# Dividing block 0's first part among three engines, with its attention in the later units' form

## The chip, the cores and the metric

The kernel runs on one core of a Trainium2 chip. TensorE (PE) multiplies matrices, and its weight loads (PEld) run beside its matmuls; VectorE (DVE), ScalarE (ACT) and GpSimd (POOL) work element by element, and SyncE (SP) issues the DMAs. Each engine works through its own instructions in the order in which they stand, and waits on semaphores for the others. The metric is the device time of one execution in microseconds; lower is better.

## The reference

```python
scores = scale * q @ k.T            # 4 batches, 8 heads, 576 tokens, head size 64
scores = where((rel >= 0) & (rel < 64), scores, -1e9)
x = softmax(scores) @ v             # -> [2304 tokens, 512]
h = x @ w_in                        # 512 -> 2048
P = a[0] + a[1]*h + a[2]*h**2 + a[3]*h**3
Q = 1 + abs(b[0])*abs(h) + abs(b[1])*h**2
x = (P / (Q + 1e-6)) @ w_out        # 2048 -> 512
out = (sigmoid(x @ w_gate) * (x @ w_val)) @ w_out2   # 512 -> 1536 -> 512
```

## The kernel before

**Tiles and phases.** The 2304 tokens are five blocks of 512, 256, 512, 512 and 512. Attention is done in 18 units of 128 tokens, four for each full block; a unit makes two score tiles (`scores`), their row maxima (`peak`), exponentials (`exps`), sums' reciprocals (`inverse`) and products (`norm`), transposes them (`turn`, `turned`), multiplies by the values (`values`) and writes x in two parts (`x_hi`, `x_lo`). "Part 1" of a block is the rational layer (`step1`, 16 values of f of 128 hidden columns each), "part 2" the gated layer (`step2`, 12 values of f). The phases run in the order part 1 and part 2 of block 0, part 1 of blocks 1 and 2, part 2 of blocks 1 and 2, and the same for blocks 3 and 4.

**Two-part numbers.** Each fp32 operand is held as a rounded part `hi` and a remainder `lo`, and each product is three matmuls (`mm3`). So a weight chunk of 128 x 512 is loaded raw (`load`, into one of three buffers of pool s) and converted once by six operations (`rescale`, `sign`, `shift`, `low_bits`, `hi`, `lo`), through a temporary `wt` in SBUF (pool t). Chunks that are needed again are stored to DRAM (`store`) and later reloaded. There are 32 chunks for part 1 (kinds i and o) and 36 for part 2 (g, v, p); pool w holds 28 at a time.

**Part 1, one f.** Twelve matmuls make `h` in one of two PSUM banks of pool h. Then come `size` and `cubic` (ACT), `slope`, `quad` (q is multiplied up), `horner` twice (DVE), `log` and `seed` (ACT), `check` (DVE), the Newton step (`newton` on DVE, or `rest` and `correct`), `ratio` (DVE), and `hi` and `lo` of the result `gs`; twelve matmuls (`product`) add it into four y banks.

**Order.** Nothing is placed by hand. Every step is given to a planner (`op`) with a priority, the engines that may do it with a cost for each (`ways`), and what it waits for; `order()` plays the program through with these costs and emits the instructions in the order that results. A cost marked `PORT` is one that the planner doesn't let overlap with another such cost on DVE or POOL. In the kernel before, most steps have two or three ways:

```python
Q = op(t0 + 1.97, [pool(n), dve(n)], quad, [Q], uses=[q_s, a_s])
X = op(t0 + 4.16, [act(n), dve2(n), pool1(n)], hi, [G], [gs_s], [g_s])
X = op(t0 + 3.61, [pool(n), dve(n)], lo, [X], uses=[gs_s, g_s])
```

**Block 0's attention.** Its four units keep q in a spare x tile and make scores from 64-row halves; later units keep q in a tile with zeros off the diagonal (`q_diag`), so that one matmul of 128 rows does for two halves. At the start the loads of q and k, of the first raw weights and, later, of v share SP's queue, in the order of the priorities.

Of the kernel before, what the change touches and what calls it, by code (L numbers as in the profile page):

```python
# [251 lines left out]
def tile_window_attention__rational_ffn__glu(  # L252
# [143 lines left out]
    def weights(c, prio, keys, again):  # L396
# [92 lines left out]
    def unit(u, t0, prio_load, prio_v):  # L489
# [37 lines left out]

        def mask_of(m):  # L530
            if first_block:
                assert (2 * u + 1) % (S // 64)
                name = "a" if 2 * u % (S // 64) == 0 else "n"
            else:
                name = "n" if (2 * u + m) % (S // 64) else "f"
            return masks[name][:, None, :].to_broadcast([P, HP, P])

        def scores(m):
            def go(e):
# [7 lines left out]
                r = slice(64 * m, 64 * m + 64)  # L547
                for i in range(HP):
                    if first_block:
                        parts = [  # L550
                            (t, z["q"][r, i, t], z["k"][r, i, t.start:t.start + P])
                            for t in (slice(0, 64), slice(64, P))
                        ]
                    else:
                        parts = [(slice(0, P), z["q"][:, 2 * i + m], z["k"][:, i, 64 * m:64 * m + P])]
                    for rows, lhs, rhs in parts:
                        nc.tensor.matmul(  # L557
                            p[rows, i * P:(i + 1) * P], lhs, rhs, start=not on_pe, stop=not on_pe or i == HP - 1
                        )
# [64 lines left out]
        def values(e):  # L624
            p = z["p"] = bank(v_s)
            for i in range(HP):
                for c in range(2):
# [86 lines left out]
    def step1(p, b, fs, f, t0):  # L714
# [366 lines left out]
```

## Time and profile before

| | |
|---|---|
| Time, three runs | 1024.28, 1024.69, 1024.74 us (median 1024.69) |
| The profiled execution: its time, its span | 1018.68 us, 1016.9 us |
| Busy in the span: PE, DVE, ACT, POOL | 960.3, 725.7, 484.8, 200.7 us |
| Moved by DMA | 170.92 MB, mean 168 GB/s |

The span is from the first to the last instruction of one profiled execution. Busy times are sums over stages that differ: the first 40 us are block 0's attention, from 40.5 us on part 1 of block 0 runs, the first matmuls of part 2 come at 204 us, and from about 400 us on PE is hardly ever idle.

### The profile page before, as it was taken

What the parts mean: (1) busy time and instruction counts of PE and PEld (TensorE: products, weight loads), DVE (VectorE), ACT (ScalarE), POOL (GpSimd) and SP (SyncE); (2) the same over time, 40 slices, a digit from 0 to 9 for tenths busy, and PEclk for the clock granted to TensorE, in tenths of its full rate; (3) what the DMA queues carried; (4) which work ended last, traced back from release to release, by engine and by line L of the source; (5) the groups of instructions that cost most, each with busy time, mean ns of one, the idle gap of its engine ahead of it and who ended that gap; (6) DMA issues with size and microseconds to landing.
All of it is one profiled execution on the core that took longest, in us unless ns stands there. A gap on an engine that the chain in (4) does not pass through costs nothing.

```text
span 1016.9 us, 14241 instructions
## 1 busy us (share of the span) xinstructions
PE 960.3 (94%) x5120; PEld 798.7 (79%) x5120; DVE 725.7 (71%) x1272; ACT 484.8 (48%) x974; POOL 200.7 (20%) x215
## 2 busy tenths in 40 slices
PE   8977777689999998999999999999999999999998
PEld 6855555468888996888998888888888888888886
DVE  5999899988888899886887765688998932222222
ACT  3775667445567874655443432565666610001001
POOL 3331232121313452231000110223232200000000
PEclk7998978699999998999999999999999999999999
DMA  9645655979999523556526675410155541005001
GB/s 291 233 145 210 245 206 197 336 257 313 318 313 345 184 68 107 197 193 223 161 63 218 211 221 179 145 63 1 47 181 188 193 158 63 1 21 186 1 1 41
DMA packets 72677, 170.92 MB, mean 168 GB/s; under 512 B 20704, under 2 KB 29920, under 8 KB 72608
## 3 DMA queue, kind: packets, MB, share of 16 engines
q1 hardware_dynamic: 72608, 170.03, 50.0%
q8 instruction: 40, 0.66, 0.3%
q14 instruction: 29, 0.24, 0.1%
HBM read 129.63 MB, written 40.37 MB: 167 GB/s over the span
## 4 chain that ended last, share of the span: by engine, by line
PE 78%; DVE 11%; DMA 6%; ACT 3%; issue 2%; POOL 0%; SPq 0%; DVEq 0%; ACTq 0%; POOLq 0%
PE h L705 29%; PE y L705 28%; PE a L705 14%; DMA wraw<-in_moe_w_out_dram 2%; DMA wraw<-in_moe_w_in_dram 2%; PE a L557 2%; DVE tg L751 2%; DVE wt L435 2%; PE a L630 1%; DVE tq L763 1%; DVE wt L430 1%; PE y L557 1%; DVE w L323 1%; PE a L380 1%; DMA qk<-in_k_dram 1%
## 5 line engine op out<-in xcount | busy, mean ns | idle before, releaser
L705 PE MATMUL h<-x,w 128*128 128x512 f32 (+1 forms) x1680 | 380.1, 376 | 15.0 <-ACT w L316 9.1
L705 PEld LDWEIGHTS h<-x,w 128*128 128x128 f32 x1680 | 299.9, 193 | 75.4 <-ACT w L316 11.7
L705 PE MATMUL y<-g,w 128*128 128x512 f32 (+1 forms) x960 | 225.9, 386 | 19.8 <-DVE g L323 11.8
L705 PEld LDWEIGHTS y<-g,w 128*128 128x128 f32 x960 | 176.0, 198 | 58.2 <-DVE g L323 14.6
L705 PE MATMUL a<-x,w 128*128 128x512 f32 (+1 forms) x720 | 160.2, 372 | 4.7 <-ACT sm L579 3.5
L705 PE MATMUL y<-w,g 128*128 128x512 f32 x648 | 158.6, 392 | 0.3 <-DVE w L323 0.3
L882 ACT ACTIVATE sg<-h 128x512 f32<-128x512 f32 (+1 forms) x60 | 33.3, 555 | 246.1 <-PE h L705 246.0
L705 PEld LDWEIGHTS a<-x,w 128*128 128x128 f32 x720 | 127.1, 190 | 28.8 <-ACT sm L579 3.9
L705 PEld LDWEIGHTS y<-w,g 128*128 128x128 f32 x648 | 120.0, 188 | 24.8 <-DVE w L323 0.6
L751 DVE SCALAR_TENSOR_TENSOR tg<-tg,ca_sb,h 128x512 f32<-128x512 f32 (+1 forms) x160 | 108.1, 688 | 24.4 <-ACT ta L730 16.6
L885 DVE TENSOR_TENSOR sg<-sg,a 128x512 f32<-128x512 f32 (+1 forms) x60 | 37.8, 633 | 121.7 <-PE a L705 118.8
L748 POOL TENSOR_TENSOR tq<-tq,ta 128x512 f32<-128x512 f32 (+1 forms) x62 | 80.4, 1299 | 123.0 <-ACT tq L739 121.5
L757 ACT ACTIVATE tr<-tq,biases 128x512 f32<-128x512 f32 (+1 forms) x80 | 54.3, 678 | 56.7 <-POOL tq L748 53.8
L734 ACT ACTIVATE tg<-h,ca_sb 128x512 f32<-128x512 f32 (+1 forms) x80 | 51.6, 645 | 52.9 <-PE h L705 52.6
L763 DVE SCALAR_TENSOR_TENSOR tq<-tq,tr 128x512 f32<-128x512 f32 (+1 forms) x80 | 54.2, 679 | 17.3 <-ACT tr L760 16.5
L427 POOL TENSOR_SCALAR wraw<-wraw 128x512 f32<-128x512 f32 x38 | 32.3, 849 | 163.4 <-ACT wt L414 151.5
L414 ACT ACTIVATE wt<-wraw 128x512 f32<-128x512 f32 x59 | 39.8, 674 | 49.0 <-DMA wraw<-in_moe_w_out_dram 24.5
L782 DVE SCALAR_TENSOR_TENSOR tg<-tg,ca_sb,tr 128x512 f32<-128x512 f32 (+1 forms) x80 | 61.9, 774 | 0.6
L768 DVE SCALAR_TENSOR_TENSOR tr<-tq,tr 128x512 f32<-128x512 f32 (+1 forms) x76 | 57.5, 760 | 0.2
L621 DVE STREAM_TRANSPOSE et<-sm 32x256 f32<-32x256 f32 x128 | 55.8, 436 | 2.3
L318 DVE CAST g<-sg 128x512 fp32r<-128x512 f32 (+1 forms) x42 | 17.1, 408 | 56.0 <-PE y L705 55.5
L760 ACT ACTIVATE tr<-tr,biases 128x512 f32<-128x512 f32 (+1 forms) x80 | 54.4, 680 | 1.8
(94 smaller groups left out, 957.0 us busy)
## 6 DMA issues: line engine op xcount, KB each, us to landing
w<-wo SPq DMA_DIRECT2D x32, 512.0 KB, 3.3
w<-wp SPq DMA_DIRECT2D x32, 512.0 KB, 3.3
wraw<-in_moe_w_out_dram SPq DMA_DIRECT2D x28, 512.0 KB, 4.7
w<-wg SPq DMA_DIRECT2D x28, 512.0 KB, 3.3
w<-wv SPq DMA_DIRECT2D x28, 512.0 KB, 3.3
w<-wi SPq DMA_DIRECT2D x20, 512.0 KB, 3.3
vv<-in_v_dram SPq DMA_DIRECT2D x35, 256.0 KB, 3.9
wraw<-in_moe_w_in_dram SPq DMA_DIRECT2D x16, 512.0 KB, 4.4
```

What stands on the lines that cost most here:

```text
L414: nc.scalar.activation(out=t.bitcast(F32), in_=x, func=AF.Copy, scale=REBIAS * REBIAS)
L621: nc.vector.transpose(out=to[cols, :, rows], in_=at[rows, :, cols])
L705: nc.tensor.matmul(p, lhs(a), rhs(b), start=first and n == 0, stop=last and n == 2)
L734: nc.scalar.activation(out=z["g"], in_=z["h"], func=AF.Copy, scale=ca_sb[:, 3:4])
L748: ENGINES[e].tensor_tensor(out=z["q"], in0=z["q"], in1=z["a"], op=ALU.mult)
L751: return lambda e: nc.vector.scalar_tensor_tensor(out=z["g"], in0=z["g"], scalar=ca_sb[:, m:m + 1], in1=z["h"], op0=ALU.add, op1=ALU.mult)
L757: nc.scalar.activation(out=z["r"], in_=z["q"], func=AF.Ln, scale=LN_SCALE, bias=lnb)
L760: nc.scalar.activation(out=z["r"], in_=z["r"], func=AF.Exp, scale=-1.0, bias=exb)
L763: nc.vector.scalar_tensor_tensor(out=z["q"], in0=z["q"], scalar=1.0 + 1e-6, in1=z["r"], op0=ALU.add, op1=ALU.mult)
L768: nc.vector.scalar_tensor_tensor(out=z["r"], in0=z["q"], scalar=2.0, in1=z["r"], op0=ALU.subtract, op1=ALU.mult, reverse0=True)
L782: nc.vector.scalar_tensor_tensor(out=z["g"], in0=z["g"], scalar=ca_sb[:, 0:1], in1=z["r"], op0=ALU.add, op1=ALU.mult)
L885: nc.vector.tensor_tensor(out=z["t"], in0=z["t"], in1=z["v"], op=ALU.mult)
```

## The change

Block 0's part 1 gets one engine for each step: `slope`, `rest` and `hi` on ACT, `quad`, `correct` and `lo` on POOL, and the Newton step is always `rest` and `correct`. The conversion of 24 of the 32 part-1 chunks (`banked`: kinds i and o from the ninth chunk on) uses a PSUM bank of pool a (two banks) as its temporary `wb` in place of `wt`, with `rescale` and `hi` on ACT, `sign` on POOL and the other three on DVE. Block 0's units take the form of the later ones, each with a tile `qd` of its own out of pool w that is cleared first; their q and k are loaded ahead of all weights, and their values go to y banks. A mask is dropped, the planner's cost of a wide matmul is raised, units of later blocks may not start before a given matmul of the phase before (`gates`), and the `hi` steps are kept in the order of f.

```diff
 def pe(n, count=1):
-    return ("PE", count * (n / 2400 + 0.0025))
+    return ("PE", count * (n / 2400 + (0.0135 if n > 256 else 0.0025)))
...
-        raw_s, t_s, w_s = Slot("s"), Slot("t"), Slot("w")
+        n = before.get("n", 0)
+        before["n"] = n + 1
+        banked = c[0] in "io" and n >= 8
+        raw_s, t_s, w_s = Slot("s"), Slot("a" if banked else "t"), Slot("w")
...
+        one, two = (dvep(512), [act(512, True)]) if banked else (dve(512), [act(512), dve2(512), pool1(512)])
         o = before["size"] = before["take"] = op(
-            prio, [act(512), dve2(512), pool1(512)], rescale, [o, before.get("size")], [t_s, w_s], [raw_s],
+            prio, two, rescale, [o, before.get("size")], [t_s, w_s], [raw_s],
...
-        o = op(prio, [pool1(512), dve2(512)], sign, [o], uses=[raw_s])
-        o = op(prio, [dve(512)], shift, [o], uses=[t_s, raw_s])
-        o = op(prio, [dve(512)], low_bits, [o], uses=[t_s, raw_s])
-        o = op(prio, [act(512), dve2(512), pool1(512)], hi, [o], uses=[t_s, w_s])
-        o = op(prio, [pool(512), dve(512)], lo, [o], uses=[t_s, w_s])
+        o = op(prio, [pool1(512)] if banked else [pool1(512), dve2(512)], sign, [o], uses=[raw_s])
+        o = op(prio, [one], shift, [o], uses=[t_s, raw_s])
+        o = op(prio, [one], low_bits, [o], uses=[t_s, raw_s])
+        o = op(prio, two, hi, [o], uses=[t_s, w_s])
+        o = op(prio, [one] if banked else [pool(512), dve(512)], lo, [o], uses=[t_s, w_s])
...
-        banks = ("y", "y", "h", "h", "a") if first_block else ("a",) * 5
+        banks = ("y", "y", "h", "h", "y") if first_block else ("a",) * 5
...
+        if first_block:
+            ready = op(-360 + u, [("NONE", 0.0)], take_q, [taken], [q_s])
+            zeros = op(-350 + u, [("DVE", 0.6, *PORT), ("POOL", 1.1, *PORT)], clear, [ready], uses=[q_s])
...
-        Q = op(t0 + 2.74, [dve2(n, 2), act(n, False, 2), pool1(n, 2)], slope, [A, coef], [q_s], [a_s])
-        Q = op(t0 + 1.97, [pool(n), dve(n)], quad, [Q], uses=[q_s, a_s])
+        Q = op(t0 + 2.74, [dve2(n, 2), act(n, False, 2), pool1(n, 2)] if b else [act(n, False, 2)], slope, [A, coef], [q_s], [a_s])
+        Q = op(t0 + 1.97, [pool(n), dve(n)] if b else [pool(n)], quad, [Q], uses=[q_s, a_s])
...
-        if b == 0 and f % 4 < 1:
-            Q = op(t0 + 0.6, [act(n, False, 1), dve2(n), pool1(n)], rest, [Q], uses=[q_s])
-            L = op(t0 + 2.52, [pool(n), dve(n)], correct, [Q], uses=[r_s, q_s])
+        if b == 0:
+            Q = op(t0 + 0.6, [act(n, False, 1)], rest, [Q], uses=[q_s])
+            L = op(t0 + 2.52, [pool(n)], correct, [Q], uses=[r_s, q_s])
...
-        X = op(t0 + 4.16, [act(n), dve2(n), pool1(n)], hi, [G], [gs_s], [g_s])
-        X = op(t0 + 3.61, [pool(n), dve(n)], lo, [X], uses=[gs_s, g_s])
+        X = prev_h["g"] = op(t0 + 4.16, [act(n), dve2(n), pool1(n)] if b else [act(n)], hi, [G], [gs_s], [g_s], prev_h.get("g"))
+        X = op(t0 + 3.61, [pool(n), dve(n)] if b else [pool(n)], lo, [X], uses=[gs_s, g_s])
...
-        unit(u, -40 + 3.48 * u, -200 + u, -200 + u + 8.94)
+        unit(u, -40 + 3.48 * u, -300 + u, -200 + u + 8.94)
```

What the planner makes of it shows in the order of the instructions. First DVE, in the middle of part 1 of block 0, before: `wt` and `w` are chunks being converted, `tg`, `tq` and `tr` the tiles of one f.

```order
163 L430 SCALAR_TENSOR_TENSOR wt<-wt,wraw 128x512
164 L748 TENSOR_TENSOR tq<-tq,ta 128x512
165 L435 SCALAR_TENSOR_TENSOR wt<-wraw,wt 128x512
166 L422 TENSOR_SCALAR wraw<-wraw 128x512
167 L318 CAST w<-wt 128x512
168 L430 SCALAR_TENSOR_TENSOR wt<-wt,wraw 128x512
169 L323 TENSOR_TENSOR w<-wt,w 128x512
170 L763 SCALAR_TENSOR_TENSOR tq<-tq,tr 128x512
171 L435 SCALAR_TENSOR_TENSOR wt<-wraw,wt 128x512
172 L782 SCALAR_TENSOR_TENSOR tg<-tg,ca_sb,tr 128x512
173 L768 SCALAR_TENSOR_TENSOR tr<-tq,tr 128x512
174 L323 TENSOR_TENSOR w<-wt,w 128x512
```

The same place on DVE after the change (lines are two lower):

```order
150 L749 SCALAR_TENSOR_TENSOR tg<-tg,ca_sb,h 128x512
151 L436 SCALAR_TENSOR_TENSOR wb<-wb,wraw 128x512
152 L749 SCALAR_TENSOR_TENSOR tg<-tg,ca_sb,h 128x512
153 L323 TENSOR_TENSOR w<-wb,w 128x512
154 L441 SCALAR_TENSOR_TENSOR wb<-wraw,wb 128x512
155 L780 SCALAR_TENSOR_TENSOR tg<-tg,ca_sb,tr 128x512
156 L323 TENSOR_TENSOR w<-wb,w 128x512
157 L436 SCALAR_TENSOR_TENSOR wb<-wb,wraw 128x512
158 L441 SCALAR_TENSOR_TENSOR wb<-wraw,wb 128x512
159 L761 SCALAR_TENSOR_TENSOR tq<-tq,tr 128x512
```

The Newton step, the remainder of `gs`, `quad` and the signs have left DVE, and the conversions read and write a PSUM bank (`wb`); ten rows make one f. Counted over the rows before part 1's result is split for part 2, DVE has 309 instructions before and 260 after, and 38 chunks are converted in both.

Next POOL, in the same part of the program, before:

```order
38 L427 TENSOR_SCALAR wraw<-wraw 128x512 x3
39 L748 TENSOR_TENSOR tq<-tq,ta 128x512
40 L427 TENSOR_SCALAR wraw<-wraw 128x512 x3
41 L748 TENSOR_TENSOR tq<-tq,ta 128x512
42 L427 TENSOR_SCALAR wraw<-wraw 128x512 x3
```

And after:

```order
73 L746 TENSOR_TENSOR tq<-tq,ta 128x512
74 L433 TENSOR_SCALAR wraw<-wraw 128x512
75 L323 TENSOR_TENSOR g<-tg,g 128x512
76 L433 TENSOR_SCALAR wraw<-wraw 128x512
77 L746 TENSOR_TENSOR tq<-tq,ta 128x512
78 L777 TENSOR_TENSOR tr<-tq,tr 128x512
79 L433 TENSOR_SCALAR wraw<-wraw 128x512 x2
80 L777 TENSOR_TENSOR tr<-tq,tr 128x512
81 L323 TENSOR_TENSOR g<-tg,g 128x512
```

POOL's share of two values of f was one `quad` and three signs; it is now two each of `quad`, `correct` and `lo`, and four signs.

Last SP, at the program's start, before:

```order
1 L405 DMA wraw<-in_moe_w_in_dram 128x1024
2 L510 DMA q_144<-in_q_dram 128x512
3 L511 DMA qk<-in_k_dram 128x4x128
4 L405 DMA wraw<-in_moe_w_in_dram 128x1024
5 L510 DMA qk<-in_q_dram 128x512
6 L511 DMA qk<-in_k_dram 128x4x128
```

And after:

```order
1 L515 DMA qd<-in_q_dram 64x8x64 x2
2 L517 DMA qk<-in_k_dram 128x4x128
3 L515 DMA qd<-in_q_dram 64x8x64 x2
4 L517 DMA qk<-in_k_dram 128x4x128
5 L515 DMA qd<-in_q_dram 64x8x64 x2
6 L517 DMA qk<-in_k_dram 128x4x128
7 L515 DMA qd<-in_q_dram 64x8x64 x2
8 L517 DMA qk<-in_k_dram 128x4x128
9 L411 DMA wraw<-in_moe_w_in_dram 128x1024 x3
```

Each q is now two DMAs of 64 rows, and the first three weight chunks stand behind all twelve loads of q and k.

## Rows read from the trace of the kernel before

**Rows 1.** Stretches: us; busy PE, PEld, DVE, ACT, POOL; granted clock, DMA share, GB/s.

```profile
0.00:40.40 40.40, 37.08 (x385) 30.83 (x386) 28.81 (x70) 20.50 (x80) 13.37 (x24) 0.83 0.77 237
40.40:206.00 165.60, 125.76 (x515) 94.27 (x513) 153.11 (x245) 107.84 (x199) 41.24 (x40) 0.85 0.65 232
206.00:320.00 114.00, 108.98 (x569) 89.72 (x564) 98.21 (x174) 67.09 (x134) 25.23 (x29) 0.99 0.91 309
320.00:400.00 80.00, 75.43 (x586) 69.45 (x585) 70.95 (x149) 54.22 (x139) 35.76 (x46) 0.96 0.44 144
400.00:1017.00 617.00, 613.10 (x3076) 514.41 (x3074) 374.61 (x638) 235.19 (x424) 85.07 (x77) 1.00 0.38 124
```

**Rows 2.** What PE waited for between 40.4 and 206 us: total, times, longest.

```profile
PE y L705 <- DVE g L323: 9.9, 6, 2.2
PE h L705 <- ACT w L316: 9.1, 5, 2.9
```

**Rows 3.** DVE's groups between 40.4 and 206 us: count, busy, mean, idle before.

```profile
L323 DVE TENSOR_TENSOR w<-wt,w 128x512 fp32r<-128x512 f32 x32 | 26.9, 858 | 2.1 <-ACT w L316 2.1
L435 DVE SCALAR_TENSOR_TENSOR wt<-wraw,wt 128x512 uint32<-128x512 uint32 x34 | 22.6, 681 | 0.0
L751 DVE SCALAR_TENSOR_TENSOR tg<-tg,ca_sb,h 128x512 f32<-128x512 f32 x32 | 22.0, 735 | 0.0
L430 DVE SCALAR_TENSOR_TENSOR wt<-wt,wraw 128x512 uint32<-128x512 uint32 x33 | 21.9, 681 | 0.0
L323 DVE TENSOR_TENSOR g<-tg,g 128x512 fp32r<-128x512 f32 x15 | 12.3, 822 | 0.0
L763 DVE SCALAR_TENSOR_TENSOR tq<-tq,tr 128x512 f32<-128x512 f32 x16 | 12.0, 750 | 7.3 <-ACT tr L760 7.2
L768 DVE SCALAR_TENSOR_TENSOR tr<-tq,tr 128x512 f32<-128x512 f32 x12 | 10.0, 833 | 0.0
L422 DVE TENSOR_SCALAR wraw<-wraw 128x512 uint32<-128x512 uint32 x13 | 5.5, 423 | 2.1 <-ACT wt L414 1.9
```

**Rows 4.** DVE in order of time from 183 us: start us, duration us, operation.

```profile
183.10 0.43 DVE L422 TENSOR_SCALAR wraw<-wraw 128x512 uint32<-128x512 uint32 x1 [0.41 <-ACT wt L414]
183.44 1.29 DVE L430 SCALAR_TENSOR_TENSOR wt<-wt,wraw 128x512 uint32<-128x512 uint32 x2
184.65 1.29 DVE L435 SCALAR_TENSOR_TENSOR wt<-wraw,wt 128x512 uint32<-128x512 uint32 x2
185.85 0.74 DVE L782 SCALAR_TENSOR_TENSOR tg<-tg,ca_sb,tr 128x512 f32<-128x512 f32 x1
```

**Rows 5.** POOL's groups between 40.4 and 206 us.

```profile
L427 POOL TENSOR_SCALAR wraw<-wraw 128x512 f32<-128x512 f32 x22 | 18.5, 839 | 109.3 <-ACT wt L414 107.5 <-DVE wt L430 1.8
L748 POOL TENSOR_TENSOR tq<-tq,ta 128x512 f32<-128x512 f32 x10 | 15.8, 1579 | 2.8 <-ACT tq L739 2.7
L323 POOL TENSOR_TENSOR g<-tg,g 128x512 fp32r<-128x512 f32 x1 | 1.3, 1295 | 0.0
```

**Rows 6.** ACT's groups between 40.4 and 206 us.

```profile
L414 ACT ACTIVATE wt<-wraw 128x512 f32<-128x512 f32 x35 | 23.6, 675 | 30.4 <-DMA wraw<-in_moe_w_out_dram 14.6 <-DMA wraw<-in_moe_w_in_dram 8.8 <-DMA wraw<-in_moe_w_gate_dram 3.4
L316 ACT CAST w<-wt 128x512 fp32r<-128x512 f32 x26 | 15.8, 616 | 12.0 <-DVE wt L435 9.7 <-DMA wg<-w 2.3
L774 ACT ACTIVATE tq<-tq,biases 128x512 f32<-128x512 f32 x3 | 2.2, 722 | 6.2 <-DVE tq L763 6.2
```

**Rows 7.** What SP's queue waited for between 40.4 and 206 us, first row.

```profile
SPq L405 <- DVE wt L435: 79.1, 29, 9.0
```

**Rows 8.** PE in order of time: part 1's fifth and sixteenth h.

```profile
58.52 4.57 PE L705 MATMUL h<-x,w 128*128 128x512 f32 x12 [4.48 <-DVE tg L751]
164.27 3.02 PE L705 MATMUL h<-x,w 128*128 128x512 f32 x12
```

**Rows 9.** DMA issues of q_diag and of unit 0's q: count, KB each, median us to landing.

```profile
q_diag<-in_q_dram SPq DMA_DIRECT2D x28, 128.0 KB, 4.0
q<-in_q_dram SPq DMA_DIRECT2D x1, 256.0 KB, 3.8
```

More of the change, by code (lines that the diff above doesn't have):

```diff
@@ L357, in constants, with off_diagonal @@
             )
-        for name, rows in (("a", 64), ("f", P)):
-            nc.vector.tensor_copy(masks[name], m)
-            nc.vector.memset(masks[name][0:rows, 0:64], MASKED)
+        nc.vector.tensor_copy(masks["f"], m)
+        nc.vector.memset(masks["f"][:, 0:64], MASKED)
         nc.vector.tensor_copy(ident16, ident)
+    def off_diagonal(engine, tile):
+        for j in range(2):
+            engine.memset(tile[64 * j:64 * j + 64, :, 64 * (1 - j):64 * (2 - j)], 0.0)
     def clear_diagonal(e):
-        for j in range(2):
-            ENGINES[e].memset(q_diag[64 * j:64 * j + 64, :, 64 * (1 - j):64 * (2 - j)], 0.0)
+        off_diagonal(ENGINES[e], q_diag)
     def coefficients(e):
@@ L408, in rescale @@
         def rescale(e):
-            t = z["t"] = temp(t_s, "wt", U32)
+            t = z["t"] = tile_of(t_s, [P, 512], U32, "wb" if banked else "wt")
             w = z["c"] = tile_of(w_s, [P, 2, 512], F32R, "w")
@@ L497, in unit @@
         k_s = spare_slot if first_block else Slot("kt")
-        q_s = Slot("w") if u == 0 else spare_slot if first_block else Slot("qt")
+        q_s = Slot("w" if first_block else "qt")
         def load_qk(e):
@@ L546, in go @@
                     nc.tensor.matmul(p, ident16, mask_of(m), start=True, stop=False)
-                r = slice(64 * m, 64 * m + 64)
                 for i in range(HP):
[L549 to L559, printed above, removed]
+                    nc.tensor.matmul(
+                        p[:, i * P:(i + 1) * P], z["q"][:, 2 * i + m], z["k"][:, i, 64 * m:64 * m + P],
+                        start=not on_pe, stop=not on_pe or i == HP - 1,
+                    )
             return go
@@ L655, in t @@
             return t0 + x
+        ready = zeros = cleared
+        if first_block:
+            ready = op(-360 + u, [("NONE", 0.0)], take_q, [taken], [q_s])
+            zeros = op(-350 + u, [("DVE", 0.6, *PORT), ("POOL", 1.1, *PORT)], clear, [ready], uses=[q_s])
         lk = op(
-            prio_load, [dma(1024 * 4 * P, 2) if first_block else dma(1792 * 4 * P, 3)], load_qk,
-            [taken if first_block else cleared],
-            [x for x in (q_s, k_s) if x is not spare_slot], {q_s, k_s}, prev_k.get("k"),
+            prio_load, [dma((1024 if first_block else 1792) * 4 * P, 3)], load_qk, [ready],
+            [x for x in (q_s, k_s) if not first_block], {q_s, k_s}, prev_k.get("k"),
         )
@@ L998, in tile_window_attention__rational_ffn__glu @@
         spans[b] = ((at[2, b - 2], at[2, b - 2] + 42), (at[2, b - 3] + 42, at[1, b - 1]))[(b - 3) % 2]
-    for b, (start, end) in spans.items():
-        for o in range(UB[b]):
-            t0 = start + o * (end - start) / UB[b] - 4.41
-            unit(U0[b] + o, t0, t0 - 1, t0)
     for n, (c, t, keys) in enumerate(fills):
@@ L1009, in tile_window_attention__rational_ffn__glu @@
     for p, (part, b, fs, t0) in enumerate(phases):
+        for x, (start, end) in spans.items():
+            if t0 <= start < t0 + (part + 1) * len(fs):
+                for o in range(UB[x]):
+                    t1 = start + o * (end - start) / UB[x] - 4.41
+                    unit(U0[x] + o, t1, t1 - 1, t1, gates.get(p))
         for i, f in enumerate(fs):
+            if i == len(fs) - 3:
+                gates[p + 1] = prev_h["h"]
             (step1, step2)[part - 1](p, b, fs, f, t0 + (part + 1) * i)
```

38 lines of the change are left out of this document (16 added, 22 removed).

## The prediction

> **What bounds the kernel now.** I read the stretches first [rows 1]. From 400 us on PE is busy 613.1 of 617 us: nothing that is done there on DVE, ACT or POOL can be seen in the time. From 206 to 400 us PE idles 5.0 and 4.6 us. The stretch that is not bound by PE is the one from 40.4 to 206 us, part 1 of block 0: PE is idle there for 39.8 of 165.6 us, and its granted clock is 0.85, a mean of stretches at 1.2 and at 2.4 GHz. The reader is to see that DVE is busy 153.1 of the 165.6 us (92%) while ACT has 107.8 and POOL 41.2. The waits say the same: PE waits mostly for `g`, which DVE's `lo` writes, and for `w` out of the conversion [rows 2], and SP holds back raw weight loads until DVE's `low_bits` frees a buffer, 79.1 us in all [rows 7]. From the fifth to the sixteenth h, 58.52 to 164.27 us [rows 8], eleven values of f take 105.8 us, 9.6 us each. So the time of this stretch is DVE's work plus its 12.5 us of idle time, and the change is worth what it takes off DVE there, as long as nothing else becomes longer.
>
> **What leaves DVE.** Four full instructions in a row start 2.41 us from the first to the one after the last (183.44 to 185.85), 0.60 us each, although one lasts 0.68; a sign takes 0.34 (183.10 to 183.44) [rows 4]. The counts are those of the order before and after, up to the end of part 1. 15 `lo` of `gs` go to POOL; their mean is 0.822 where an unlengthened instruction of this kind takes 0.681 (`shift` and `low_bits`), so each costs 0.60 + 0.14: 11.1 us [rows 3]. 12 Newton steps become `rest` on ACT and `correct` on POOL: 12 x (0.60 + 0.15) = 9.0. 6 `quad`, 4 `correct` and 2 `norm` at 0.60: 7.2. 7 signs, one `rest` and 2 short casts at 0.34: 3.4. In all 30.7 us. The 32 `lo` of chunks have a mean of 0.858, 0.177 over 0.681, 5.7 us together [rows 3]; the `horner` steps, which read one operand from PSUM, run at 0.735 with POOL busy a quarter of the time and show no such lengthening as the SBUF-only ones do. 24 of the 33 `lo` after the change read a PSUM bank, so I take off three quarters of the 5.7: 4.3. Sum: 35.0 us, 153.1 to 118.1.
>
> **What comes in its place.** POOL gets 16 each of `quad`, `correct` and `lo` at 1.295 (62.2), 29 signs at 0.839 (24.3) [rows 5] and keeps 5.6 of other work: 92 us, 66% of a stretch of 140 us in place of 25%. DVE instructions that work in SBUF alone are held up by it. Before, the five SBUF-only kinds lose 5.7 + 2.1 + 1.8 + 1.1 us over the unlengthened 0.681, the two conversion steps nothing: 10.7 us over 142 instructions, 0.075 each [rows 3]. With POOL 2.65 times as busy I take 0.20. After, 62 are exposed: 16 `check`, 16 `ratio`, and three each of some ten unbanked chunks: 12.4 us, of which 2.7 are in the sum already. DVE: 118.1 + 9.7 = 127.8. The bounds of this price: nothing more than now (118.1), and double (140). No row shows DVE writing PSUM, as `shift` and `low_bits` now do; the nearest, `horner`, which reads it, is 0.05 longer with its extra scalar operand, so I take nothing, and 48 x 0.05 = 2.4 as the upper end.
>
> **ACT** gets 13 `rest` at 0.722 and a few more casts, about 11 us: 107.8 to 119. It is idle for 57.8 us of the stretch now, so this lies beside other work if ACT's idle time shrinks to 21 us; most of it are waits of `rescale` for a raw load (30.4 us) and of `hi` for `low_bits` (12.0) [rows 6], which are late because DVE is late. **The port** of the costs marked PORT would be taken for POOL's 92 plus 62 x 0.60 = 37 us on DVE, 129 in all: it is the next bound, 11 us below.
>
> **Sum.** If DVE keeps its 12.5 us of idle time, the stretch takes 127.8 + 12.5 = 140.3 us in place of 165.6: 25 us less. If it idles for the 14% that it does from 206 to 320 us (15.8 of 114, [rows 1]), 149 us, 17 less; with no new waits 130.6, 35 less.
>
> **The edits with no price.** The first 40.4 us are taken as they are, from 3 us longer to 5 shorter: the same bytes of q, k, v and weights go through; weights come later but are first needed by the h at 40.5 us, and six operations of some 0.7 us stand between; eight clears on DVE lie in its idle time ahead of the first maxima (DVE is busy 28.8 of 40.4). For q in two halves the rows show 128 KB landing in 4.0 us, where unit 0's 256 KB took 3.8 [rows 9]: the pieces cost about a second transfer's latency, and 8 in place of 4. By the Trainium skill (DMA: Bandwidth & Descriptors, the table of specifications) a transfer below 512 B doesn't reach line rate, and q now lands in pieces of 256 B; an estimate by it, 1 MB at half of the 237 GB/s of [rows 1], would put 4.4 us on the start and give 1004. Behind 206 us the order moves, but work stays: PE's idle 5.0 and 4.6 us are all there is to gain, and as much I allow for loss. The bytes of the stretch, 232 GB/s x 165.6 us = 38.4 MB, go through 140 us at 274 GB/s, less than the 309 from 206 to 320 us.
>
> **Time.** The profiled execution took 1018.68 us, 1.8 more than its span; 25 less is 993.7. The runs' median is 6.0 us above it, and since I know no reason why that should change, I take the 25 from the median: 999.7 us.
>
> **The rivals.**
> (a) ACT takes DVE's place. Its order is fixed: a `rescale` that stands waiting for its load holds up `cubic`, `log` and `seed` behind it, and DVE and PE wait for those. If its idle time falls by a third only, to 38.5 us, the stretch is 119 + 38.5 = 157.5 us: 8 less, 1016.7. For it speaks that its waits for loads come from three raw buffers, which stay three; against it, that the buffers are freed by DVE.
> (b) Slower. Each banked chunk holds one of two PSUM banks of pool a from `rescale` to `lo`, where eleven SBUF buffers were shared before, and one f uses up two chunks: an f can't take less than the time T that a chunk holds its bank. With 9.6 us per f now [rows 8] it decides from T = 9.6; at 10.6 the eleven f cost 11 us more, 1035.7. The six operations alone are 0.675 + 0.839 + 0.60 + 0.60 + 0.616 + 0.60 = 3.9 us; T has to stay under 7.3 for the forecast, so 3.4 us of standing in five queues are free.
> (c) Given back. Part 2 of block 0 needs 36 new chunks, with DMA at 0.91 [rows 1]. If those that now load ahead in the slow stretch are then missing, PE waits from 206 us on for what was won: 1024. Against it: the order converts as many chunks, 38, before part 1 ends.
> (d) Moving work to POOL doesn't help at all, because DVE stands still while POOL runs: 118.1 + 92 = 210 us, 45 more, 1069. The rows speak against it: `low_bits` has a mean of 0.681 and `horner` of 0.735 with POOL busy [rows 3]. The Trainium skill (Perfetto Trace Analysis, Optimizing Scalar/DVE Operations) warns of this very thing, that moving work between GpSimd and DVE might not help since they share an SBUF port; the trace agrees only for the instructions that work in SBUF alone.
> (e) More than forecast: DVE's idle time goes too, the start is shorter, and PE's clock stays high: 47 us or more, below 978.
>
> **How the numbers follow.** Forecast 0.61 (its own range 985 to 1010), (a) 0.19, (b) 0.08, (c) 0.05, (d) 0.02, (e) 0.05. The range from 978 to 1018 holds the forecast and (a), and leaves out 0.20. No change that could be told from none is 0.2%, 2 us. Faster are forecast, (a) and (e): 0.85; same is (c): 0.05; slower (b) and (d): 0.10.
>
> **What would show it.** In the changed kernel's stretches the first h starts near 40 us and the first matmuls of part 2 near 179, with DVE busy some 128 us between; from the fifth to the sixteenth h an f takes 7 to 8 us; `lo` of chunks has a mean near 0.68, `check` and `ratio` lie above it, POOL is busy 90 us. Under (a) ACT's waits of `rescale` for loads stay near 30 us; under (b) `rescale` waits for the `lo` of the chunk before the last; under (c) PE idles after part 2's start. Wrong would be an f of over 9 us, or PE idle behind part 1.

## The result, and the profile after

| | before | after |
|---|---|---|
| Time, median of four runs each on one chip | 1024.72 us (1024.28 to 1026.61) | 991.55 us (991.27 to 991.62) |
| Ratio, 95% interval | | 0.9697 (0.9658 to 0.9736) |
| Profiled execution: time, span | 1018.68, 1016.9 us | 991.5, 989.6 us |
| First h | 40.46 us | 38.20 us |
| First matmul of part 2 | 204.11 us | 182.77 us |
| From there to the end | 812.8 us | 806.8 us |

The change takes 33.2 us off the median and 27.3 off the profiled span: 2.3 ahead of the first h, 19.1 between the first h and part 2, 6.0 behind. The rest of the 33.2 is the profiled execution of before, 6.0 below its own median.

The stretches of the changed kernel (columns as in [rows 1]):

```profile
0.00:38.10 38.10, 30.58 (x307) 27.83 (x308) 26.02 (x66) 20.16 (x80) 16.73 (x28) 0.96 0.77 226
38.10:182.70 144.60, 112.24 (x513) 80.96 (x511) 131.62 (x198) 115.62 (x216) 96.26 (x86) 0.96 0.78 271
182.70:206.00 23.30, 18.05 (x74) 14.39 (x69) 19.62 (x38) 11.31 (x21) 3.06 (x3) 0.85 0.72 261
```

Part 1 of block 0 takes 144.6 us, with DVE busy 131.6, ACT 115.6 and POOL 96.3. From the first matmul of part 2 to the end, before and after:

```profile
204.11:1016.90 812.79, 799.39 (x4260) 675.05 (x4258) 545.66 (x962) 357.22 (x697) 147.35 (x154) 0.99 0.46 152
182.77:989.60 806.83, 795.16 (x4229) 671.83 (x4225) 542.16 (x959) 359.29 (x703) 134.25 (x142) 1.00 0.46 153
```

PE idles 11.7 us there in place of 13.4, and is busy 4.2 us less, with 31 fewer matmuls on record. So of the 6.0 us won behind part 1 only 1.7 are idle time; what the rest is made of isn't settled. Right behind part 1 PE still idles 5.3 of 23.3 us.

PE in order of time, part 1's fifth and sixteenth h and part 2's first, against [rows 8]:

```profile
52.30 0.50 PE L703 MATMUL h<-x,w 128*128 128x512 f32 x1 [1.81 <-ACT ta L728]
...
141.15 0.39 PE L703 MATMUL h<-x,w 128*128 128x512 f32 x1
...
182.77 0.50 PE L703 MATMUL h<-x,w 128*128 128x512 f32 x1
```

Eleven values of f take 88.85 us, 8.1 each; before it was 9.6. DVE's groups between the first h and part 2, against [rows 3] (here `shift` is L436 and `low_bits` L441):

```profile
L749 DVE SCALAR_TENSOR_TENSOR tg<-tg,ca_sb,h 128x512 f32<-128x512 f32 x32 | 23.6, 739 | 2.2 <-ACT ta L728 1.1 <-ACT tg L732 0.8
L436 DVE SCALAR_TENSOR_TENSOR wb<-wb,wraw 128x512 uint32<-128x512 uint32 x24 | 16.4, 689 | 0.9 <-POOL wraw L433 0.9
L441 DVE SCALAR_TENSOR_TENSOR wb<-wraw,wb 128x512 uint32<-128x512 uint32 x24 | 16.4, 686 | 0.2
L323 DVE TENSOR_TENSOR w<-wb,w 128x512 fp32r<-128x512 f32 x24 | 16.3, 681 | 0.2 <-ACT w L316 0.2
L761 DVE SCALAR_TENSOR_TENSOR tq<-tq,tr 128x512 f32<-128x512 f32 x16 | 15.0, 941 | 4.5 <-ACT tr L758 4.5
L780 DVE SCALAR_TENSOR_TENSOR tg<-tg,ca_sb,tr 128x512 f32<-128x512 f32 x16 | 14.4, 901 | 0.0
L441 DVE SCALAR_TENSOR_TENSOR wt<-wraw,wt 128x512 uint32<-128x512 uint32 x11 | 9.7, 882 | 0.1
```

The reader sees two classes. What has an operand in PSUM (`wb`, and h for `horner`) lasts 0.68 to 0.74 us; what works in SBUF alone (`check` L761, `ratio` L780, `low_bits` of `wt`) lasts 0.88 to 0.94, and the other two steps on `wt` 0.82 and 0.85. POOL's three new kinds of work, against [rows 5]:

```profile
L746 POOL TENSOR_TENSOR tq<-tq,ta 128x512 f32<-128x512 f32 x16 | 22.3, 1394 | 5.8 <-ACT tq L737 5.8
L323 POOL TENSOR_TENSOR g<-tg,g 128x512 fp32r<-128x512 f32 x16 | 21.6, 1352 | 7.5 <-ACT g L316 7.5
L777 POOL TENSOR_TENSOR tr<-tq,tr 128x512 f32<-128x512 f32 x16 | 20.8, 1299 | 4.4 <-ACT tq L772 4.4
```

PE's waits between the first h and part 2, against [rows 2]: total, times, longest.

```profile
PE a L600 <- POOL sm L589: 7.0, 1, 7.0
PE y L703 <- ACT w L316: 5.9, 5, 2.6
PE y L703 <- POOL g L323: 2.8, 3, 1.0
```

The waits for `g` fall from 9.9 to 2.8 us and are short now. The first row stands at 174 us; the same wait took 4.2 us in the profile of before (`PE a L604 <- POOL sm L593: 4.2, 1, 4.2`). ACT and POOL in order of time just ahead of it:

```profile
171.14 0.62 ACT L420 ACTIVATE wb<-wraw 128x512 f32<-128x512 f32 x1 [2.63 <-DMA wraw<-in_moe_w_out_dram]
```

```profile
171.91 0.65 POOL L433 TENSOR_SCALAR wraw<-wraw 128x512 f32<-128x512 f32 x1 [1.71 <-ACT wb L420]
172.52 2.47 POOL L589 TENSOR_TENSOR sm<-sm,su 128x512 f32<-128x512 f32 x2
```

`norm` (L589) stands in POOL's queue behind a sign, the sign behind a `rescale` that waits for its raw load. From the sixteenth h to part 2 the changed kernel takes 41.6 us, 1.8 more than before.

### The profile page after: what moved, and what is told of

It is laid out like the page before. It is cut to its first block, busy times and chain, and to the rows that moved or that the text cites. A ratio compares the mean times of both kernels' runs of the same rounds, so it can differ in the third digit from the quotient of the medians.

```text
span 989.6 us, 14065 instructions
## 1 busy us (share of the span) xinstructions
PE 938.0 (95%) x5042; PEld 780.6 (79%) x5042; DVE 699.9 (71%) x1221; ACT 495.1 (50%) x999; POOL 247.2 (25%) x255
## 4 chain that ended last, share of the span: by engine, by line
PE 72%; DVE 9%; DMA 8%; ACT 6%; issue 2%; POOL 1%; SPq 1%; DVEq 0%; POOLq 0%; ACTq 0%
PE y L703 28%; PE h L703 27%; PE a L703 13%; DMA wraw<-in_moe_w_out_dram 4%; PE a L552 2%; DVE w L323 2%; DMA wraw<-in_moe_w_in_dram 1%; DVE tg L749 1%; DVE wt L441 1%; PE a L626 1%; DMA wraw<-in_moe_w_val_dram 1%; ACT tr L755 1%; SPq L515 1%; DVE tq L761 1%; DVE wb L436 1%
## 5 line engine op out<-in xcount | busy, mean ns | idle before, releaser
L703 PE MATMUL h<-x,w 128*128 128x512 f32 (+1 forms) x1680 | 372.1, 370 | 9.3 <-DVE w L323 4.0
L703 PEld LDWEIGHTS h<-x,w 128*128 128x128 f32 x1680 | 292.6, 189 | 69.5 <-DVE w L323 7.9
L703 PE MATMUL y<-g,w 128*128 128x512 f32 (+1 forms) x960 | 217.3, 375 | 12.0 <-ACT w L316 5.9
L703 PEld LDWEIGHTS y<-g,w 128*128 128x128 f32 x960 | 168.5, 191 | 49.4 <-ACT w L316 7.9
L746 POOL TENSOR_TENSOR tq<-tq,ta 128x512 f32<-128x512 f32 (+1 forms) x54 | 71.7, 1329 | 56.4 <-ACT tq L737 44.2
L755 ACT ACTIVATE tr<-tq,biases 128x512 f32<-128x512 f32 (+1 forms) x80 | 53.9, 676 | 38.0 <-POOL tq L746 34.6
L761 DVE SCALAR_TENSOR_TENSOR tq<-tq,tr 128x512 f32<-128x512 f32 (+1 forms) x80 | 57.1, 713 | 17.1 <-ACT tr L758 16.6
L780 DVE SCALAR_TENSOR_TENSOR tg<-tg,ca_sb,tr 128x512 f32<-128x512 f32 (+1 forms) x80 | 64.4, 806 | 0.8
L741 POOL TENSOR_SCALAR tq<-ta,cb_sb 128x512 f32<-128x512 f32 (+1 forms) x27 | 21.2, 785 | 153.9 <-ACT ta L728 150.7
L433 POOL TENSOR_SCALAR wraw<-wraw 128x512 f32<-128x512 f32 x42 | 34.0, 811 | 69.1 <-ACT wt L420 19.1
L728 ACT ACTIVATE ta<-h 128x512 f32<-128x512 f32 (+1 forms) x80 | 43.9, 550 | 5.4 <-DVE tg L749 5.4
```

The costliest lines, as they stand in the source:

```text
L433: nc.gpsimd.tensor_scalar(out=x, in0=x, scalar1=0.0, scalar2=0.0, op0=ALU.mult, op1=ALU.mult)
L703: nc.tensor.matmul(p, lhs(a), rhs(b), start=first and n == 0, stop=last and n == 2)
L728: nc.scalar.activation(out=z["a"], in_=z["h"], func=AF.Abs)
L746: ENGINES[e].tensor_tensor(out=z["q"], in0=z["q"], in1=z["a"], op=ALU.mult)
L755: nc.scalar.activation(out=z["r"], in_=z["q"], func=AF.Ln, scale=LN_SCALE, bias=lnb)
L761: nc.vector.scalar_tensor_tensor(out=z["q"], in0=z["q"], scalar=1.0 + 1e-6, in1=z["r"], op0=ALU.add, op1=ALU.mult)
```

## The experiments

The first theory is the prediction's: the steps that move take 30.7 us off DVE, and the banks' share is the smaller one (4.3 us for `lo`, and 72 instructions that needn't pay the 0.20 each). Its rival: the banks are what counts, because a DVE instruction that has an operand in PSUM isn't held up by POOL, and without them the division gains nothing. All runs were timed beside the kernel before on the same chip; ratios are to that.

**The kernel before once more.**

> The kernel before once more, to see its runs with span and granted clock. Theory: its profiled execution (1018.7 us, clock 0.963) and its other runs (1024.3 to 1026.6) differ in how long TensorE ran at 1.2 GHz, so the other runs show a mean clock lower than 0.963 and 5 to 8 us more span. Rival: a profiled execution is simply shorter by 6 us, at the same clock; then all clocks agree within 0.003 and the changed kernel's profiled execution (991.5, like its other runs) is the odd one.

Measured: 1022.34 us (1014.43 to 1027.2), ratio 0.9965 (0.9935 to 0.9995). The kernel before varies by 13 us by itself, mostly along with its mean granted clock: 1014.43 us at 0.970, 1021.05 at 0.967, 1024.48 at 0.962, 1027.2 at 0.958. That is the theory; the rival, a shorter time at the same clock, fell. Two sets of runs of one kernel thus differ by 0.35%, and smaller differences say nothing. The first stretch of its fastest run, against the first row of [rows 1]:

```profile
0.00:35.50 35.50, 32.37 (x385) 27.31 (x386) 27.80 (x69) 20.19 (x80) 12.85 (x24) 1.00 0.85 270
```

At a granted clock of 1.00 in place of 0.83 the first h comes at 35.59 us in place of 40.46; the rest of the two runs takes the same time within 1 us (1012.6 - 35.59 = 977.0 and 1016.9 - 40.46 = 976.4).

**The bank taken away, nothing else.** Every engine has the same instructions in the same order.

```diff
-            t = z["t"] = tile_of(t_s, [P, 512], U32, "wb" if banked else "wt")
+            t = z["t"] = pools["t"].tile([P, 512], U32, tag="t", name="wb" if banked else "wt")
```

> The changed kernel with the 24 banked temporaries in SBUF, every instruction in the same place. Theory (SBUF-only DVE instructions are held up by a busy POOL): 72 more of them are exposed at 0.2 us each, 14 us: about 1006 us, and the means of shift, low_bits and lo of these chunks rise from 0.68-0.69 to 0.85-0.9. Rival (the banks matter only as room): within 2 us of 991.6, means as they were.

Measured: 1015.34 us, ratio 0.992 (0.989 to 0.995), 23.8 above the changed kernel. The stretch from the first h to part 2, and DVE's groups in it:

```profile
36.70:206.50 169.80, 121.39 (x512) 86.04 (x510) 159.01 (x197) 117.49 (x216) 110.28 (x86) 0.92 0.64 230
```

```profile
L441 DVE SCALAR_TENSOR_TENSOR wb<-wraw,wb 128x512 uint32<-128x512 uint32 x24 | 29.1, 1218 | 0.2
L436 DVE SCALAR_TENSOR_TENSOR wb<-wb,wraw 128x512 uint32<-128x512 uint32 x24 | 26.8, 1118 | 0.0
...
L323 DVE TENSOR_TENSOR w<-wb,w 128x512 fp32r<-128x512 f32 x24 | 20.5, 854 | 0.7 <-ACT w L316 0.6
```

The 72 instructions whose operand moved to SBUF cost 27.3 us more (76.4 in place of 49.1), 0.38 each, where 0.20 and 14 us were expected. DVE's busy time grows by 27.4, the stretch by 25.2, the time by 23.8. POOL's instructions in the stretch get longer too, by 14.0 us (110.3 in place of 96.3). How the two hold each other up shows in order of time:

```profile
102.25 1.60 POOL L323 TENSOR_TENSOR g<-tg,g 128x512 fp32r<-128x512 f32 x1 [1.94 <-ACT g L316]
102.64 1.75 DVE L436 SCALAR_TENSOR_TENSOR wb<-wb,wraw 128x512 uint32<-128x512 uint32 x1
103.81 1.73 POOL L777 TENSOR_TENSOR tr<-tq,tr 128x512 f32<-128x512 f32 x1
104.32 0.73 DVE L749 SCALAR_TENSOR_TENSOR tg<-tg,ca_sb,h 128x512 f32<-128x512 f32 x1
```

DVE's `shift`, all in SBUF, ends at 104.39, 0.54 us behind the end of POOL's `lo`; POOL's `correct`, which starts beside it, takes 1.73 us in place of 1.30; and `horner`, which reads h from PSUM, takes its usual 0.73 beside `correct`. Only the place of the temporary differs between the two kernels, so the hold-up is what makes the stretch longer.

**The division with and without the banks.** Four kernels: the kernel before with the division of the steps alone; the changed kernel with the ways of `step1` as before; the kernel before with the banked conversion alone (the lines on `weights`, nothing else); the changed kernel without banks.

```diff
-        Q = op(t0 + 1.97, [pool(n), dve(n)], quad, [Q], uses=[q_s, a_s])
+        Q = op(t0 + 1.97, [pool(n), dve(n)] if b else [pool(n)], quad, [Q], uses=[q_s, a_s])
...
-        X = op(t0 + 3.61, [pool(n), dve(n)], lo, [X], uses=[gs_s, g_s])
+        X = op(t0 + 3.61, [pool(n), dve(n)] if b else [pool(n)], lo, [X], uses=[gs_s, g_s])
```

> The kernel before with step 1's fixed division alone. Theory (without the banks all conversions are exposed to a busy POOL, 134 instructions at 0.2 us): 27 us off DVE, some 20 more of waits: 1015 to 1021 us. Rival (the division does it all by itself): 998 to 1003 us. Other rival (POOL's port holds DVE up for all that is moved): 1025 or more.

> The changed kernel with step 1's ways as before (banks, units and loads stay). Theory (the division takes some 27 us of work off DVE, which bounds): DVE's busy time in part 1 of block 0 rises from 132 to about 150 us and the time to 1008-1013 us. Rival (banks, start and later order did it): below 997 us.

```diff
-        raw_s, t_s, w_s = Slot("s"), Slot("t"), Slot("w")
+        banked = c[0] in "io" and n >= 8
+        raw_s, t_s, w_s = Slot("s"), Slot("a" if banked else "t"), Slot("w")
```

> The kernel before with the 24 banked conversions alone. Theory (with the temporaries out of SBUF the planner's own choice moves quad, lo and the signs to POOL, and nothing on DVE is held up; the fixed division is not needed): DVE's busy time in the slow stretch falls from 151-153 to about 138 us, and the time to 998-1008. Rival (the gain needs the banks and the other parts together): 1012 or more.

```diff
-        banked = c[0] in "io" and n >= 8
+        banked = False
```

> The changed kernel without banks: all temporaries in pool t, everything else as changed. Theory (a busy POOL costs each SBUF-only DVE instruction 0.2 to 0.4 us, and 134 are exposed): like the kernel with the temporaries in SBUF, 1010 to 1022. Rival (it was the fixed order, planned for banks, that made that one slow; planned anew it does without): under 1003.

| | median us | ratio, 95% interval |
|---|---|---|
| Division alone | 1031.3 | 1.0073 (1.0037 to 1.0108) |
| The change without banks | 1027.84 | 1.0038 (1.0007 to 1.0068) |
| Banks alone | 992.87 | 0.9714 (0.9663 to 0.9766) |
| The change without division | 992.24 | 0.9692 (0.9655 to 0.9729) |
| The change | 991.55 | 0.9697 (0.9658 to 0.9736) |

With banks 992, without them 1028 to 1031, whoever does the steps. None of the four theories' ranges was hit: the two kernels with banks came out faster than theirs, the two without slower. For the division alone and for the change without it the figures are those of a rival (1025 or more; below 997). The stretches of the change without division and of the change without banks:

```profile
37.40:188.50 151.10, 117.66 (x512) 88.05 (x510) 137.40 (x214) 99.52 (x190) 80.21 (x84) 0.90 0.73 261
37.40:222.50 185.10, 131.88 (x480) 93.36 (x479) 158.77 (x212) 120.61 (x216) 89.36 (x64) 0.82 0.58 208
```

Without the division the stretch takes 6.5 us more than in the changed kernel, with DVE busy 137.4 us (150 were expected), but the time is the same. Without banks the time is 12.5 us above that of the kernel that has the changed kernel's order and its temporaries in SBUF (ratio 1.0038 against 0.992). DVE is busy 159 us in both, but idles 26.3 us in place of 10.8: told of the shared port for every chunk, the planner made another order, with 23 signs on DVE in place of 6. So of the 36 us between the changed kernel and the one without banks about 24 are the hold-up, and 12 go with the order. Division alone, the stretch and DVE's groups:

```profile
34.61:216.20 181.59, 132.34 (x480) 93.72 (x479) 154.80 (x207) 120.08 (x216) 87.49 (x62) 0.82 0.57 207
```

```profile
L435 DVE SCALAR_TENSOR_TENSOR wt<-wraw,wt 128x512 uint32<-128x512 uint32 x33 | 27.8, 860 | 0.0
L430 DVE SCALAR_TENSOR_TENSOR wt<-wt,wraw 128x512 uint32<-128x512 uint32 x33 | 27.7, 856 | 0.1
...
L422 DVE TENSOR_SCALAR wraw<-wraw 128x512 uint32<-128x512 uint32 x23 | 20.4, 890 | 5.3 <-ACT wt L414 5.3
L763 DVE SCALAR_TENSOR_TENSOR tq<-tq,tr 128x512 f32<-128x512 f32 x16 | 11.8, 737 | 10.1 <-ACT tr L760 10.0
```

The steps did leave DVE, and yet it is busy 154.8 us. The two conversion steps, 0.681 in [rows 3], last 0.86 beside a POOL that is busy 87 us: 66 times 0.177 is 11.7 us. The signs cost 20.4 us in place of 5.5, since POOL is too full for them (23 in place of 13) and each is held up (0.890 in place of 0.423). These 26.6 us take back most of what left, and DVE's idle time grows from 12.5 to 26.8 us, 10.0 of it before `check`, which waits for ACT's `seed`.

Without the division the planner, which has both ways, moves work to POOL of its own accord once the banked costs aren't marked PORT: with banks alone POOL gets 15 `quad`, 6 `lo` and 4 `correct` of gs up to the end of part 1, where it had 10, 1 and none. The next run asks how much of the banks' gain is that.

**Banks, but with their costs marked PORT,** so that the planner moves less.

```diff
-        one, two = (dvep(512), [act(512, True)]) if banked else (dve(512), [act(512), dve2(512), pool1(512)])
+        one, two = (dve(512), [act(512, True)]) if banked else (dve(512), [act(512), dve2(512), pool1(512)])
```

> The banked conversion alone, as in banks_only, but the planner is told that the banked shift, low_bits and lo cost the shared port as before, so it hands less to POOL: up to the end of part 1 it puts some 298 instructions on DVE where banks_only has 282 and the kernel before 309, and POOL gets 8 quad, 4 lo and 3 correct of gs where banks_only has 15, 6 and 4. Theory 1 (the banks gain because DVE loses work to POOL): 16 instructions of 0.6 us stay on DVE, some 10 us of the gain of 32, about 1003 us. Theory 2 (the banks gain because 72 instructions on DVE no longer wait for POOL, whoever has the other work): within 4 us of banks_only, 990 to 997 us.

Measured: 1001.75 us (997.14 to 1006.01), ratio 0.9797 (0.9752 to 0.9841). The stretch from the first h to part 2 in this kernel, and behind it in the one with banks alone:

```profile
42.55:194.94 152.39, 120.45 (x512) 85.14 (x510) 140.24 (x227) 103.23 (x196) 49.86 (x51) 0.92 0.68 246
```

```profile
43.08:191.73 148.65, 121.18 (x521) 89.53 (x520) 136.31 (x216) 101.70 (x199) 76.62 (x78) 0.89 0.72 255
```

Both theories hold a part: by the ratios the banks are worth 2.0% while POOL stays nearly as free as before (49.9 us), and 2.9% where the work moves too (76.6 us). 1001.75 us is near what the first theory gave, but that theory counts 10 us only. The intervals overlap (0.9752 to 0.9766), and in the kernel with marked costs too DVE has fewer instructions in the stretch than before (227 against 242 from the first h to part 2), so the split into about 21 and 9 us is rough.

**The other parts of the change.** The planner's cost, gates and the order of the `hi` steps as before; then block 0's attention and loads as before.

```diff
-    return ("PE", count * (n / 2400 + (0.0135 if n > 256 else 0.0025)))
+    return ("PE", count * (n / 2400 + 0.0025))
...
-                    unit(U0[x] + o, t1, t1 - 1, t1, gates.get(p))
+                    unit(U0[x] + o, t1, t1 - 1, t1)
```

> The changed kernel with the old cost of a wide matmul, no gates and no order of the hi steps. Theory (these edits touch what comes after part 1 of block 0, where 6 us were gained that the prediction didn't have): part 1 as in the changed kernel within 3 us, and 3 to 6 us lost behind it, 994 to 998. Rival (the 6 us come from part 1's better state, not from these edits): 990.5 to 993. Other rival (units that start early disturb part 1): 1000 or more.

```diff
-        banks = ("y", "y", "h", "h", "y") if first_block else ("a",) * 5
+        banks = ("y", "y", "h", "h", "a") if first_block else ("a",) * 5
```

> The changed kernel with block 0's attention and its loads as before. Theory (the start is bounded by the same bytes and the same chain): the first h comes 0 to 4 us later and nothing else changes, 991.5 to 996. Rival (loading q and k first is worth more, since TensorE then doesn't fall to 1.2 GHz in the start): the first h 5 us or more later, 997 or more.

Measured: 987.97, 989.91 and 990.24 us (ratio 0.9669, 0.9613 to 0.9725) and 991.08 us (ratio 0.9677, 0.9625 to 0.9729). Neither part is worth anything that these runs can tell. Part 2 starts at 188.19 and 187.58 us in them, some 5 us later than in the changed kernel, and they end no later: those 5 us are given back behind, where PE idles 7.4 and 8.6 us in place of 11.7.

**What bounds the stretch now.** Work left out: one `horner` of every f on DVE, then `rest` on ACT.

```diff
-            return lambda e: nc.vector.scalar_tensor_tensor(
+            return lambda e: None if b == 0 and m == 1 else nc.vector.scalar_tensor_tensor(
```

> The changed kernel, leaving out the second horner of every gs of block 0 (16 instructions of DVE at 0.66 to 0.74 us, about 11 us; the output lacks that term). Every other instruction is in its place. Theory 1 (DVE still bounds the stretch up to the first matmuls of part 2 after the change, idle 13.0 of 144.6 us): 8 to 11 us less than the changed kernel, 981 to 984 us. Theory 2 (something else, ACT's order or the raw loads, bounds it now): 0 to 4 us less, 987 to 992 us.

```diff
+            if b == 0:
+                return
```

> The changed kernel, leaving out the operation rest of every gs of block 0 (up to 16 instructions, most on ACT, about 10 us; the output lacks that part of the Newton step). Every other instruction is in its place. Theory 1 (DVE bounds the stretch): 0 to 3 us less than the changed kernel, 988 to 992 us. Theory 2 (ACT bounds it, busy 115.6 of 144.6 us and held by waits in its fixed order): 7 to 10 us less, 982 to 985 us.

Measured: 991.72 us (990.2 to 993.05), nothing, and 989.55 us (989.21 to 990.45), 2.0 less. The theory that DVE still bounds the stretch fell, and so did the one that ACT does. The stretch without one `horner`, and DVE's groups in it:

```profile
36.63:182.27 145.64, 114.37 (x513) 82.34 (x511) 125.06 (x183) 115.61 (x216) 95.98 (x86) 0.94 0.75 271
```

```profile
L761 DVE SCALAR_TENSOR_TENSOR tq<-tq,tr 128x512 f32<-128x512 f32 x16 | 15.8, 986 | 6.9 <-ACT tr L758 6.9
L780 DVE SCALAR_TENSOR_TENSOR tg<-tg,ca_sb,tr 128x512 f32<-128x512 f32 x16 | 15.8, 985 | 0.0
```

DVE has 6.6 us less to do and idles 7.6 more, and its SBUF-only steps last longer. ACT's `rescale` without `rest` waits 7.9 us for DVE's `lo` where it had 3.9 in the changed kernel:

```profile
L420 ACT ACTIVATE wb<-wraw 128x512 f32<-128x512 f32 x24 | 15.3, 637 | 11.5 <-DVE w L323 7.9 <-DMA wraw<-in_moe_w_out_dram 1.9 <-DMA wraw<-in_moe_w_in_dram 1.6
```

That `lo` frees the PSUM bank. The changed kernel in order of time, ACT's `rescale` into a bank and DVE's `lo` out of it:

```profile
105.30 0.65 ACT L420 ACTIVATE wb<-wraw 128x512 f32<-128x512 f32 x1 [1.28 <-DVE w L323]
108.38 0.63 ACT L420 ACTIVATE wb<-wraw 128x512 f32<-128x512 f32 x1
111.80 0.63 ACT L420 ACTIVATE wb<-wraw 128x512 f32<-128x512 f32 x1
115.74 0.64 ACT L420 ACTIVATE wb<-wraw 128x512 f32<-128x512 f32 x1
120.07 0.63 ACT L420 ACTIVATE wb<-wraw 128x512 f32<-128x512 f32 x1 [1.31 <-DVE w L323]
```

```profile
104.59 0.68 DVE L323 TENSOR_TENSOR w<-wb,w 128x512 fp32r<-128x512 f32 x1
106.92 0.68 DVE L323 TENSOR_TENSOR w<-wb,w 128x512 fp32r<-128x512 f32 x1
110.98 0.68 DVE L323 TENSOR_TENSOR w<-wb,w 128x512 fp32r<-128x512 f32 x1
114.99 0.68 DVE L323 TENSOR_TENSOR w<-wb,w 128x512 fp32r<-128x512 f32 x1
119.36 0.68 DVE L323 TENSOR_TENSOR w<-wb,w 128x512 fp32r<-128x512 f32 x1
```

Each `rescale` takes the bank that the `lo` before it has left: 104.59 + 0.68 is 105.27, and the next starts at 105.30; 111.66 and 111.80, 115.67 and 115.74, 120.04 and 120.07 (only at 108.38 does the bank stand empty, for 0.78 us). A chunk holds its bank from `rescale` to the end of `lo`: 6.36, 7.29 and 8.24 us for the three that begin at 105.30, 108.38 and 111.80. Two chunks an f on two banks, 14.77 us for two f (105.30 to 120.07): 7.4 us an f. It is the same from the third banked chunk to the twentieth: nine turns of one bank take 65.3 us (71.78 to 137.10), nine of the other 66.6 (74.54 to 141.10), and from the fifth chunk on a bank stands empty for at most 0.78 us between two of them. With one `horner` left out the nine turns take 65.2 and 66.4 us, without `rest` 65.9 and 67.1. So in this part the banks turn over almost without a pause, and work left out on one engine becomes a wait of the chunk in another's queue. Behind 141 us a bank stands empty for 4 to 15 us before its next chunk, so the last 41.6 us of the stretch have another bound. That the banks are the bound in between is read from the trace and not shown: DVE is busy 64.7 us, ACT 62.8 and POOL 53.9 of the 69.3 us from 71.78 to 141.10, and neither a third bank nor less work on POOL was tried.

**Four more chunks in banks.**

```diff
-        banked = c[0] in "io" and n >= 8
+        banked = c[0] in "io" and n >= 4
```

> The changed kernel with the temporaries of input and output chunks in banks from the fifth chunk on in place of the ninth. Four more chunks lie in banks, twelve instructions fewer on DVE wait for POOL, at 0.2 to 0.38 us each 2 to 5 us. Theory 1 (exposure to POOL still costs): 986 to 989 us. Theory 2 (those chunks are converted in the first 40 us, where DVE has idle time, or the banks of pool a get short there): 991 us or up to 4 more.

Measured: 991.52 us (986.66 to 992.83), ratio 0.9684: no change. No version beat the changed kernel by more than the runs can tell.

## Why the prediction came out as it did

The forecast of 999.7 us was 8.1 above the result, inside its own range. That it came so near is partly luck: the stretch gave 6 us less than forecast, and 14 us came from where the forecast has zero. Step by step:

- **DVE bounds the stretch: likely for before.** From the first h to part 2 DVE's work falls from 151.2 to 136.3 us with banks alone, and the stretch from 163.65 to 148.65: 14.9 and 15.0 us. With the bank taken from the changed kernel, the stretch grows by 25.2 us and DVE's work by 27.4. Both fit, but no run changed DVE's work in the kernel before and nothing else. For after, "the time of this stretch is DVE's work plus its 12.5 us of idle time" no longer holds: with 6.6 us less work on DVE (11.8 us of `horner` left out, 5.2 back in longer instructions) the stretch takes 145.6 us in place of 144.6.
- **What leaves DVE: the step that failed.** It put 30.7 us down to steps that move and 4.3 to the banks. By the runs the division by itself gains nothing (0.7% slower, where the kernel before differs from itself by 0.35%), and banks alone nearly all of it. The prediction priced the banks by the one instruction, `lo`, that was visibly held up in [rows 3], and in the next step by leaving 72 instructions out of the 0.20 each, 14 us; they cost 27.3. `shift` and `low_bits`, at 0.681 in [rows 3], were not held up with POOL busy 41 us. They are with POOL busy 87 us (0.86), and it is the banks that keep them at 0.69.
- **What comes in its place: right in sum.** `check` and the unbanked chunks above 0.681, and `ratio` above the 0.74 of [rows 4], cost 11.7 us, forecast 12.4; DVE 131.6 us, forecast 127.8; POOL 96.3 for 92; ACT 115.6 for 119. The 0.20 us an instruction is no constant, though: with all of them exposed the 72 pay 0.38 each. (The losses that it adds up as those of five kinds are of four.)
- **Sum: 140.3 us forecast, 144.6 measured.** (Its bound with 14% of idle time comes to 148 us, not 149.) Less was won in the stretch (19.1 of 25 us), 2.3 ahead of it and 6.0 behind, where the prediction had zero, with bounds of 5 us ahead and 9.6 behind. The 4.4 us that half the rate for q in 256-byte pieces would have put on the start didn't come: the eight loads of 128 KB land in 3.8 us (median), and the first h comes earlier. The 25 were taken off the median, "since I know no reason why that should change". It did change: the changed kernel's profiled execution lies at its median, and 6.0 us of the 33.2 are that. Why its runs spread less isn't settled; two profiles of before only show that its first 40 us come at either 0.83 or 1.00 of the clock.
- **Rival (a), ACT:** didn't come. `rescale` waits 10.9 us for loads (4.6 into `wb`, 6.3 into `wt`), where [rows 6] has 26.8 of its 30.4 put down to them, and ACT's work without `rest` gave 2.0.
- **Rival (b), the banks of pool a:** its mechanism is there, at a smaller price. "T has to stay under 7.3 for the forecast"; the banks turn over in 7.3 to 7.4 us an f from 72 to 141 us, under the 9.6 from which it would have cost time. It is what the trace points to as the next bound there.
- **Rival (c), given back:** not for the whole, but for the last 5 us, as the kernels that start part 2 at 188 us show. Its sign, which was also one of being wrong, is there in small: PE idles 5.3 us of the first 23.3 behind part 1.
- **Rival (d), moving work to POOL doesn't help:** refuted for the change; for the division alone right in kind (1031.3 us), far below its price (1069). The rule of the Trainium skill (Perfetto Trace Analysis, Optimizing Scalar/DVE Operations) that such moves might not help agrees with that run; the trace adds what makes them help, an operand in PSUM.

## What to carry to other kernels

Before work is moved from DVE to POOL, count the DVE instructions that stay and have all operands in SBUF: each can be held up, and that can take back the whole gain. A free PSUM bank as the temporary of a chain of element-wise steps took them out of POOL's way here, and the planner, told of it, then moved work by itself. When a change has two parts that each look like the gain, run each alone before saying which it was; and when two banks are shared by a chain, look whether one turn is as long as the loop.

## What the runs showed of the hardware

- The same DVE instruction (`shift`, `low_bits`) with POOL busy 67 and 65% of the stretch: 0.69 us with its temporary in PSUM, 1.12 and 1.22 with all of it in SBUF. The hold-up goes both ways: POOL's `lo` of gs rises from 1.352 to 1.560 us and `correct` from 1.299 to 1.535 when the banks are taken away. The Trainium skill (SBUF — State Buffer, SBUF: two separate sides) says that a DVE operation with two SBUF inputs and a GpSimd operation that reads SBUF exclude each other for a whole instruction; the trace agrees (a `shift` ended 0.54 us behind POOL's `lo`), and one input in PSUM was enough to be free of it.
- DVE writing PSUM costs 0.686 to 0.689 us for 128 x 512, hardly more than the 0.681 into SBUF of [rows 3]; the prediction had allowed up to 0.05 more.
- The kernel before ran between 1014.4 and 1029.0 us on the chips used, mostly the longer the lower its mean granted clock was (0.970 at 1014.43 us, 0.955 at 1029.01), but not always (0.973 at 1026.22).
